# Preparing the inputs of the Strassen passes later in the plain steps

## The chip, the core and the metric
The kernel runs on one core of a Trainium2 chip. The metric is the device time of one execution in microseconds (us). The engines are called PE (TensorE matrix multiply), DVE (VectorE), ACT (ScalarE), POOL (GpSimd) and SP (SyncE, which here only issues transfers); PEld is the weight load of TensorE.

## The reference, cut to what matters
An attention block is followed by two feed-forward layers. The change lies in the second one, on 2304 tokens with 512 features and 1536 hidden columns:

```python
def _moe2_ref(x, w_gate, w_val, w_out, rms_g) -> np.ndarray:
    rms = np.sqrt(np.mean(x * x, axis=-1, keepdims=True) + 1e-06)
    xn = x / rms * rms_g
    g = xn @ w_gate
    silu = g * (1.0 / (1.0 + np.exp(-g)))
    val = xn @ w_val
    return (silu * val @ w_out).astype(np.float32)
```

## The kernel before, in words
Every product is made of three matmuls on split numbers: each operand is a high part (a cast on ACT) and a low part (a subtraction on DVE). Weights arrive as raw words (`raw`), are put together by two ACT operations (L184, L186) and one of DVE (L196, `ct`), and are then split into high (L203, ACT) and low (L207, DVE), tile `w`.

The second layer begins with a **plain part**, a loop over f = 0 to 11 (line 1385 and below), one step for each 128 hidden columns, on the first 256 tokens. A step prepares weights two steps ahead (`st2.to`), multiplies the 256 tokens by the gate and the value weight of step f (`pe_gv`: 12 matmuls each into `ps_h`), makes the activation (`s`, then its high and low part `p`: L949 ACT, L950 DVE, L952 ACT, L953 DVE), and adds the product with the output weight of step f - 2 (`pe_o`: 6 matmuls into `ps_x`).

The other 2048 tokens go through **Strassen passes** on sums and differences of weights. Their token inputs are seven tiles `xt`, one per product, numbered 1, 2, 5, 6, 3, 7, 4. A call of the generator `pg` in the plain loop runs `conv` for one of them: for numbers 5, 6, 7 and 4 a subtraction on DVE (L1039, `tr`, 128 x 1024), then for each a cast on ACT (L1058) and a subtraction on DVE (L1059). The same plain steps start the weight sums for the passes (`decode`): loads `wa`, sums `ws` on POOL (L302) and their split `wo` on POOL (L285, L286). The first pass reads tile 1 (`ps_pr<-xt,wt`) near the end of the plain part.

Who goes first is decided in two ways. From the last attention group on, transfers on SP go out in the order of the program. The instructions of PE, DVE, ACT and POOL in the plain part are put in order by the scheduler of the framework when the program is built: it plays the program through on its own estimate of times and takes, on each engine, the ready instruction that stands earliest in the program, unless `tc.high_priority` moves one forward (the activation of each step has it). On the chip every engine then keeps that order.

Of the kernel before, what the change touches and what calls it, by code (L numbers as in the profile page):

```python
# [34 lines left out]
def attn_moe_moe_kernel(  # L35
# [25 lines left out]
    B, _, NC, D = q_str.shape  # L61
    NT, DM = out.shape
    FA = w_in.shape[0]
    FB = w_gate.shape[0]
# [16 lines left out]
    def runs(s):  # L81

        r = []
        for i, (b, t) in enumerate(subs[s]):
            if r and r[-1][0] == b and r[-1][1] + r[-1][2] == t:
                r[-1][2] += 64
            else:
                r.append([b, t, 64, 64 * i])
        return r
# [36 lines left out]
    for s in range(len(subs)):  # L126
        if len(runs(s)) > 1 or s in LANES:
            _, t0, n, _ = runs(s)[0]
# [808 lines left out]
    def pe_gv(j, f):  # L937
        r, n = [], R0
        bank = (bank_h, bank_m, bank_h, bank_m, bank_x, bank_x)[f % 6]("ps_h")
        for k, kd in enumerate(("gate", "val")):  # L940
            ps = bank[:, k * n:k * n + n]
            w, x = w2[kd, f].t, xn[j]
            seq = [(a, e, c) for c in range(4) for a, e in ((0, 0), (0, 1), (1, 0))]
            for i, (a, e, c) in enumerate(seq):
                mm(ps, w[:, a, c, :], x[:, e, c, :], i == 0, i == len(seq) - 1)
            r.append(ps)
        with tc.high_priority(400):
            s = pb.tile([128, n], F32, tag="s", name="s", bufs=3)
            nc.scalar.activation(out=s, in_=r[0], func=ACTF.Silu, scale=WS)  # L949
            nc.vector.scalar_tensor_tensor(out=s, in0=r[1], scalar=WS, in1=s, op0=ALU.mult, op1=ALU.mult)  # L950
            t = pb.tile([128, 2, n], F32R, tag="p", name="p", bufs=3)
            nc.scalar.copy(out=t[:, 0], in_=s)  # L952
            nc.vector.tensor_tensor(out=t[:, 1], in0=s, in1=t[:, 0].bitcast(F32), op=ALU.subtract)  # L953
        p_of[j, f] = t

    def pe_o(j, f):
        if f == 0:
            oacc[j] = [ps_x.tile([128, 512], F32, tag="x", name="ps_x") for _ in range(R0 // 128)]
        w, p = w2["out2", f].t.rearrange("p s c f -> p s (c f)"), p_of.pop((j, f))
        for t in range(R0 // 128):  # L960
            for i, (a, e) in enumerate(((0, 0), (1, 0), (0, 1))):
                mm(
                    oacc[j][t], p[:, e, t * 128:t * 128 + 128], w[:, a, :],
                    f == 0 and i == 0, f == FB - 1 and i == 2,
                )
# [422 lines left out]
    for f in range(FB):  # L1388
        if f == FB - 4:
            pairs[0].fetch((0, 1))  # L1390
        st2.to(max(3 * (f + 2), N1 + (len(w2_order) - N1) * (f + 1) // (FB - 2)))
        store.plain(st2.i - 1)
        store.to(st2.i - 6)
        pe_gv(0, f)
        for _ in range(3 if f < FB - 2 else 40):
            next(pg, None)
        decode.to(max(0, min(8, 8 * (f - 4) // 6)))
        if f > 1:
            pe_o(0, f - 2)
# [155 lines left out]
```

## Time and profile before

| what | us |
|---|---|
| median of 3 runs (lowest, highest) | 886.05 (885.49, 890.01) |
| the profiled execution, its own time | 887.88 |
| its span in the trace | 886.1 |
| PE busy in that span | 866.5 |

The mean clock granted to PE over the span is 0.992 of full. Times in the rows below are microseconds from the start of the span. A busy PE is not PE at its peak, since matmuls overlap; what counts is where PE stood idle, and what it waited for. The plain part lies at about 470 to 522 us.

### The profile page before, as it was taken

The page shows a single profiled execution, that of the slowest core. Times are in us where ns is not written, and L with a number is a line of the kernel's source. Part 1 is how long each engine was busy: PE and PEld are TensorE (multiplying, and loading weights), DVE is VectorE, ACT ScalarE, POOL GpSimd, SP SyncE. Part 2 cuts the span into 40 slices and gives each one's busy share as a digit, 9 for nine tenths or more (in the row PEclk, how much of TensorE's full clock was granted, in tenths as well). Part 3 has the DMA queues.
Part 4 walks back from the last instruction along what each step waited for, and adds up shares of the span by engine and source line. Part 5 has one row for each costly group of instructions (what it writes and reads, how often), then busy time and mean ns, then how long its engine had stood idle before and what let it go on. Part 6 is the DMA issues. An engine that isn't in the chain of part 4 may idle for free.

```text
span 886.1 us, 14047 instructions
## 1 busy us (share of the span) xinstructions
PE 866.5 (98%) x5091; PEld 722.7 (82%) x5091; DVE 629.8 (71%) x1290; ACT 413.9 (47%) x916; POOL 250.6 (28%) x309
## 2 busy tenths in 40 slices
PE   7999999999999999999999899999999999999998
PEld 4888888888998887888889877888788888888886
DVE  5999778888779887657778945569688553445544
ACT  6887633333543333878657644533325324322230
POOL 0000147695366853000000679846200000000000
PEclk8999999999999999999999999999999999999999
DMA  9965224311313000889977999765661288544002
GB/s 302 368 223 178 74 75 156 104 57 36 115 55 110 25 19 27 330 306 370 412 252 227 352 372 336 299 230 214 211 216 48 75 320 353 177 149 136 1 1 95
DMA packets 63717, 164.12 MB, mean 185 GB/s; under 512 B 10080, under 2 KB 21728, under 8 KB 63648
## 3 DMA queue, kind: packets, MB, share of 16 engines
q1 hardware_dynamic: 61088, 159.56, 51.1%
q10 hardware_dynamic: 2560, 3.67, 1.2%
q8 instruction: 40, 0.66, 0.3%
q14 instruction: 29, 0.24, 0.1%
HBM read 119.16 MB, written 44.04 MB: 184 GB/s over the span
## 4 chain that ended last, share of the span: by engine, by line
PE 58%; DVE 10%; POOL 7%; issue 2%; ACT 2%; DMA 1%; SPq 0%; ACTq 0%; DVEq 0%; POOLq 0%
PE ps_pr L150 20%; PE ps_o L150 14%; PE ps_h L150 10%; PE ps_x L150 9%; POOL pr L675 5%; DVE so L715 4%; PE ps_q L150 4%; POOL pr L708 1%; DVE tg L860 1%; DVE g L871 1%; DMA wt<-w 1%; DMA w<-w 1%; DVE s L1108 0%; DVE sm L451 0%; POOL ws L302 0%
## 5 line engine op out<-in xcount | busy, mean ns | idle before, releaser
L150 PE MATMUL ps_h<-xs,w 128*128 128x512 f32 (+1 forms) x984 | 214.6, 367 | 0.7 <-DVE tg L860 0.7
L150 PE MATMUL ps_x<-g,w 128*128 128x512 f32 (+1 forms) x984 | 214.2, 366 | 0.0
L150 PEld LDWEIGHTS ps_h<-xs,w 128*128 128x128 f32 x984 | 169.9, 190 | 30.5 <-DVE tg L860 1.3
L150 PEld LDWEIGHTS ps_x<-g,w 128*128 128x128 f32 x984 | 168.5, 189 | 30.4 <-ACT g L866 0.4
L150 PE MATMUL ps_pr<-xt,wt 128*128 128x512 f32 x576 | 137.6, 390 | 2.0 <-DVE s L1118 1.1
L150 PE MATMUL ps_o<-wt,p 128*128 128x512 f32 x576 | 136.0, 389 | 0.0
L150 PEld LDWEIGHTS ps_pr<-xt,wt 128*128 128x128 f32 x576 | 107.7, 188 | 26.2 <-DVE s L1118 2.0
L150 PEld LDWEIGHTS ps_o<-wt,p 128*128 128x128 f32 x576 | 108.1, 188 | 22.5
L675 POOL TENSOR_TENSOR pr<-sk,sq 128x256 f32<-128x256 f32 (+2 forms) x101 | 82.6, 852 | 133.0 <-DMA sq<-in_q_str_dram 107.3
L866 ACT CAST g<-tg 128x512 fp32r<-128x512 f32 (+1 forms) x82 | 46.5, 567 | 101.3 <-DVE tg L860 101.2
L1129 ACT COPY u<-ps_pr 128x512 f32<-128x512 f32 x72 | 41.9, 587 | 103.5 <-PE ps_pr L150 103.4
L708 POOL TENSOR_TENSOR pr<-sv,se 128x288 f32<-128x288 f32 (+12 forms) x104 | 69.7, 691 | 57.0 <-DVE so L715 19.8
L1181 DVE SCALAR_TENSOR_TENSOR osum<-ps_o,osum 128x512 f32<-128x512 f32 x80 | 54.8, 687 | 27.2 <-PE ps_o L150 26.6
L302 POOL TENSOR_TENSOR ws<-wa 128x256 f32<-128x256 f32 x24 | 24.6, 1044 | 170.4 <-DVE w L207 152.2
L715 DVE TENSOR_REDUCE so<-pr 128x16 f32<-128x272 f32 (+11 forms) x104 | 64.9, 653 | 9.0 <-POOL pr L708 8.6
L150 PE MATMUL ps_pr<-xt,wo 128*128 128x512 f32 x288 | 67.4, 389 | 0.0
L150 PEld LDWEIGHTS ps_pr<-xt,wo 128*128 128x128 f32 x288 | 54.1, 188 | 11.3
L871 DVE TENSOR_TENSOR g<-tg,g 128x512 fp32r<-128x512 f32 (+1 forms) x82 | 55.3, 676 | 10.6 <-ACT g L866 9.3
L860 DVE SCALAR_TENSOR_TENSOR tg<-ps_h,tg 128x512 f32<-128x512 f32 (+1 forms) x82 | 50.6, 618 | 15.9 <-ACT tg L855 15.6
L855 ACT ACTIVATE tg<-ps_h 128x512 f32<-128x512 f32 (+1 forms) x82 | 44.2, 540 | 34.8 <-PE ps_h L150 34.7
L196 DVE SCALAR_TENSOR_TENSOR ct<-ca,ct 128x512 uint32<-128x512 uint32 x68 | 48.0, 713 | 16.6 <-ACT ca L186 16.0
L680 DVE TENSOR_REDUCE sc<-pr 128x4 f32<-128x256 f32 (+2 forms) x101 | 43.7, 437 | 12.1 <-POOL pr L675 11.7
(121 smaller groups left out, 1045.7 us busy)
## 6 DMA issues: line engine op xcount, KB each, us to landing
wt<-w SPq DMA_DIRECT2D x84, 512.0 KB, 4.6
w<-w SPq DMA_DIRECT2D x36, 512.0 KB, 6.2
raw<-in_w_out_dram SPq DMA_DIRECT2D x28, 512.0 KB, 5.8
w<-wo SPq DMA_DIRECT2D x24, 512.0 KB, 7.4
raw<-in_w_in_dram SPq DMA_DIRECT2D x16, 512.0 KB, 8.6
raw<-in_w_gate_dram SPq DMA_DIRECT2D x12, 512.0 KB, 6.7
raw<-in_w_val_dram SPq DMA_DIRECT2D x12, 512.0 KB, 7.1
wa<-v SPq DMA_DIRECT2D x24, 256.0 KB, 4.7
```

Source lines behind the costliest of these rows:

```text
L150: nc.tensor.matmul(out_, lhsT, rhs, start=start, stop=stop, skip_group_check=True)
L196: nc.vector.scalar_tensor_tensor(out=t, in0=self.a.bitcast(U32), scalar=3, in1=t, op0=ALU.logical_shift_left, op1=ALU.bitwise_or)
L675: nc.gpsimd.tensor_tensor(out=pr, in0=self.k[:, a:e, :], in1=self.q[:, c - c0:c - c0 + 1, :].to_broadcast([128, e - a, D]), op=ALU.mult,)
L680: pend.append(lambda: nc.vector.tensor_reduce(out=s[:, c - c0, a:e], in_=pr, axis=AX.X, op=ALU.add))
L708: nc.gpsimd.tensor_tensor(out=pr, in0=self.v[:, 0:c + 1, a:e], in1=self.e[:, c - c0, 0:c + 1].unsqueeze(2).to_broadcast([128, c + 1, e - a ...
L715: pend.append(lambda: nc.vector.tensor_reduce(out=o[:, c - g0, a:e], in_=pr.rearrange("l c d -> l d c"), axis=AX.X, op=ALU.add))
L855: nc.scalar.activation(out=t, in_=h_of[g, f, a], func=ACTF.Tanh, scale=WS)
L860: nc.vector.scalar_tensor_tensor(out=t, in0=h_of.pop((g, f, a)), scalar=WS, in1=t, op0=ALU.mult, op1=ALU.subtract)
L866: nc.scalar.copy(out=t[:, 0], in_=t_of[g, f, a])
L871: nc.vector.tensor_tensor(out=t[:, 1], in0=t_of.pop((g, f, a)), in1=t[:, 0].bitcast(F32), op=ALU.subtract)
L1129: nc.scalar.copy(out=u, in_=x[kd])
L1181: nc.vector.scalar_tensor_tensor(out=o, in0=ps, scalar=WS, in1=o, op0=ALU.mult, op1=ALU.add)
```

## The change
In each of the plain steps 0, 1 and 2 the loop called `next(pg)` three times, so all seven `conv` (the last two calls found nothing left) were in the program there. Now steps 0 to 3 call it not at all, step 4 twice (numbers 1 and 2) and steps 5 to 9 once (5, 6, 3, 7, 4). No instruction is added or removed; what moves is the place of 18 of them in the program, and with it the order that the scheduler finds.

```diff
         pe_gv(0, f)
-        for _ in range(3 if f < FB - 2 else 40):
+        for _ in range((f >= 4) + (f == 4) if f < FB - 2 else 40):
             next(pg, None)
         decode.to(max(0, min(8, 8 * (f - 4) // 6)))
```

The next two pieces are the order on DVE behind the L1059 of `xt1` and `xt2`, at about 483 us of the program before. Gate and value weight of step 7 are `w_5773` and `w_5778` before, `w_5765` and `w_5770` now; `xt_5706` is the tile shared by the numbers 3 and 7; `tr` are the differences. Before:

```order
L1039 TENSOR_TENSOR tr_5815<-x2_5239,tr_5762 128x1024
L1039 TENSOR_TENSOR tr_5821<-x2_5239 128x1024
L1059 TENSOR_TENSOR xt_5706<-x2_5239,xt_5706 128x1024
L207 TENSOR_TENSOR w_5773<-ct_5721,w_5773 128x512
L196 SCALAR_TENSOR_TENSOR ct_5827<-ca_5829,ct_5827 128x512
L1059 TENSOR_TENSOR xt5_5703<-tr_5762,xt5_5703 128x1024
L950 SCALAR_TENSOR_TENSOR s_5973<-ps_h_5948,s_5973 128x256
L207 TENSOR_TENSOR w_5778<-ct_5768,w_5778 128x512
L196 SCALAR_TENSOR_TENSOR ct_5877<-ca_5879,ct_5877 128x512
L950 SCALAR_TENSOR_TENSOR s_6014<-ps_h_5989,s_6014 128x256
L1059 TENSOR_TENSOR xt6_5704<-tr_5815,xt6_5704 128x1024
L1059 TENSOR_TENSOR xt_5706<-tr_5821,xt_5706 128x1024
```

The same place on DVE of the changed program:

```order
L1059 TENSOR_TENSOR xt_5706<-x2_5239,xt_5706 128x1024
L207 TENSOR_TENSOR w_5765<-ct_5721,w_5765 128x512
L207 TENSOR_TENSOR w_5770<-ct_5760,w_5770 128x512
L950 SCALAR_TENSOR_TENSOR s_5952<-ps_h_5927,s_5952 128x256
L196 SCALAR_TENSOR_TENSOR ct_5809<-ca_5811,ct_5809 128x512
L1059 TENSOR_TENSOR xt5_5703<-tr_6003,xt5_5703 128x1024
L196 SCALAR_TENSOR_TENSOR ct_5856<-ca_5858,ct_5856 128x512
L950 SCALAR_TENSOR_TENSOR s_5997<-ps_h_5972,s_5997 128x256
L950 SCALAR_TENSOR_TENSOR s_6064<-ps_h_6039,s_6064 128x256
L953 TENSOR_TENSOR p_5955<-s_5952,p_5955 128x256
L207 TENSOR_TENSOR w_5861<-ct_5809,w_5861 128x512
```

The two `tr` and the two L1059 of numbers 6 and 7 are gone from here; the weights of steps 7 and 8 (`w_5861`, before `w_5882`) come earlier.

They stand further down, ahead of the weights of step 10, which are `w_6033` (gate) and `w_6087` (value) in the changed program. DVE of the changed program there:

```order
L1039 TENSOR_TENSOR tr_6070<-x2_5239,tr_6070 128x1024
L196 SCALAR_TENSOR_TENSOR ct_6021<-ca_6023,ct_6021 128x512
L953 TENSOR_TENSOR p_6188<-s_6185,p_6188 128x256
L1059 TENSOR_TENSOR xt4_5705<-tr_6070,xt4_5705 128x1024
L207 TENSOR_TENSOR w_6033<-ct_6021,w_6033 128x512
L950 SCALAR_TENSOR_TENSOR s_6231<-ps_h_6206,s_6231 128x256
L1039 TENSOR_TENSOR tr_6191<-x2_5239 128x1024
L953 TENSOR_TENSOR p_6234<-s_6231,p_6234 128x256
L196 SCALAR_TENSOR_TENSOR ct_6028<-ca_6030,ct_6028 128x512
L1059 TENSOR_TENSOR xt_5706<-tr_6191,xt_5706 128x1024
L207 TENSOR_TENSOR w_6087<-ct_6028,w_6087 128x512
```

The value weight of step 10 now has `s_6231` and `p_6234` (activation of step 9) ahead of it, and `tr` and `xt` of number 7 as its neighbours.

PE at the end of the plain part, before (`w_6046`, `w_6096` are the weights of step 10, `w_6161`, `w_6204` those of step 11, `p_6279` the activation of step 10, `w_6039` its output weight):

```order
L150 MATMUL ps_h_6251<-xn_5193,w_6096 128x256 x10
L150 MATMUL ps_x_5868<-w_5776,p_6195 128x512
L150 MATMUL ps_x_5867<-w_5885,p_6237 128x512 x2
L150 MATMUL ps_x_5868<-w_5885,p_6237 128x512 x2
L150 MATMUL ps_x_5867<-w_5885,p_6237 128x512
L150 MATMUL ps_x_5868<-w_5885,p_6237 128x512
L150 MATMUL ps_h_6294<-xn_5193,w_6161 128x256 x2
L150 MATMUL ps_pr_6342<-xt1_5701,wt_6143 128x512 x6
L150 MATMUL ps_x_5867<-w_6039,p_6279 128x512 x2
L150 MATMUL ps_x_5868<-w_6039,p_6279 128x512 x2
L150 MATMUL ps_h_6294<-xn_5193,w_6161 128x256 x10
```

PE of the changed program from the value weight of step 10 on (`w_6154` and `w_6201` are the weights of step 11):

```order
L150 MATMUL ps_h_6251<-xn_5193,w_6087 128x256 x12
L150 MATMUL ps_x_5846<-w_6026,p_6279 128x512 x2
L150 MATMUL ps_x_5847<-w_6026,p_6279 128x512 x2
L150 MATMUL ps_x_5846<-w_6026,p_6279 128x512
L150 MATMUL ps_x_5847<-w_6026,p_6279 128x512
L150 MATMUL ps_pr_6342<-xt1_5701,wt_6136 128x512 x6
L150 MATMUL ps_h_6294<-xn_5193,w_6154 128x256 x12
L150 MATMUL ps_pr_6349<-xt1_5701,wt_6138 128x512 x6
L150 MATMUL ps_h_6294<-xn_5193,w_6201 128x256 x12
```

The output product of step 10 follows directly on the matmuls whose result it needs (`p_6279` is made from `ps_h_6251`); before, 15 other matmuls stood between. The order of transfers on SP and on ACT's queue is the same in both programs.

## Rows read from the trace of the kernel before

**Rows 1.** The page: busy time and share of each engine.

```profile
PE 866.5 (98%) x5091; PEld 722.7 (82%) x5091; DVE 629.8 (71%) x1290; ACT 413.9 (47%) x916; POOL 250.6 (28%) x309
```

**Rows 2.** Waits of PE, 482 to 545: total us, times, longest.

```profile
PE ps_h L150 <- DVE w L207: 2.1, 2, 1.8
PE ps_x L150 <- ACT p L952: 1.8, 2, 1.4
```

**Rows 3.** Waits of PE from 545 to the end.

```profile
PE ps_pr L150 <- DVE s L1118: 0.4, 1, 0.4
```

**Rows 4.** Timeline of PE: start, us, instruction, count, idle before.

```profile
487.10 2.25 PE L150 MATMUL ps_h<-xn,w 128*128 128x256 f32 x14 [0.30 <-DVE w L207]
...
493.90 2.26 PE L150 MATMUL ps_h<-xn,w 128*128 128x256 f32 x12 [1.84 <-DVE w L207]
```

**Rows 5.** Windows: busy us of PE, PEld, DVE, ACT, POOL; clock; DMA share; GB/s.

```profile
491.90:493.90 2.00, 0.17 (x2) 0.00 (x0) 2.00 (x4) 0.41 (x2) 0.00 (x0) 1.00 1.00 297
493.90:496.10 2.20, 2.19 (x13) 2.20 (x14) 2.20 (x5) 1.61 (x4) 0.67 (x1) 0.69 1.10 366
496.10:498.50 2.40, 2.40 (x9) 1.86 (x8) 2.40 (x5) 2.12 (x3) 2.40 (x1) 0.57 0.88 243
498.50:502.00 3.50, 3.50 (x25) 3.14 (x24) 3.50 (x4) 2.52 (x5) 3.50 (x4) 1.00 1.02 398
```

**Rows 6.** The chain that ended last: start, us, engine, tile, count.

```profile
493.90 2.26 PE ps_h L150 x12
496.17 2.37 PE ps_x L150 x6
...
500.42 1.40 PE ps_x L150 x6
501.81 1.42 PE ps_h L150 x12
...
508.63 1.19 PE ps_h L150 x10
...
511.80 1.37 PE ps_pr L150 x6
```

**Rows 7.** Timeline of DVE, first to last of the stretch before POOL starts.

```profile
478.00 0.69 DVE L196 SCALAR_TENSOR_TENSOR ct<-ca,ct 128x512 uint32<-128x512 uint32 x1
...
490.57 2.35 DVE L1059 TENSOR_TENSOR xt<-tr,xt 128x1024 fp32r<-128x1024 f32 x2
...
493.17 0.68 DVE L207 TENSOR_TENSOR w<-ct,w 128x512 fp32r<-128x512 f32 x1
```

**Rows 8.** Timeline of POOL, its first row of the plain part.

```profile
495.43 4.71 POOL L302 TENSOR_TENSOR ws<-wa 128x256 f32<-128x256 f32 x2 [152.24 <-DVE w L207]
```

**Rows 9.** Timeline of DVE while POOL works.

```profile
499.47 1.76 DVE L1059 TENSOR_TENSOR xt<-tr,xt 128x1024 fp32r<-128x1024 f32 x1
501.15 1.23 DVE L207 TENSOR_TENSOR w<-ct,w 128x512 fp32r<-128x512 f32 x1
...
504.33 0.41 DVE L950 SCALAR_TENSOR_TENSOR s<-ps_h,s 128x256 f32<-128x256 f32 x1
...
505.48 0.95 DVE L953 TENSOR_TENSOR p<-s,p 128x256 fp32r<-128x256 f32 x1
506.36 1.22 DVE L207 TENSOR_TENSOR w<-ct,w 128x512 fp32r<-128x512 f32 x1
```

**Rows 10.** Timeline of PE, the last output product of the plain part.

```profile
519.98 1.66 PE L150 MATMUL ps_x<-w,p 128*128 128x512 f32 x6 [1.43 <-ACT p L952]
```

**Rows 11.** Timeline of ACT: the value weight of step 11.

```profile
512.79 0.77 ACT L184 ACTIVATE ct<-raw,colf 128x512 uint32<-128x512 uint16 x1 [1.24 <-DMA raw<-in_w_val_dram]
...
515.36 0.62 ACT L203 CAST w<-ct 128x512 fp32r<-128x512 f32 x1 [1.24 <-DVE ct L196]
```

**Rows 12.** Timeline of DVE: the same weight.

```profile
514.16 1.17 DVE L196 SCALAR_TENSOR_TENSOR ct<-ca,ct 128x512 uint32<-128x512 uint32 x1 [1.11 <-ACT ca L186]
516.02 1.02 DVE L207 TENSOR_TENSOR w<-ct,w 128x512 fp32r<-128x512 f32 x1 [0.69 <-ACT w L203]
```

## The prediction, made before the changed kernel ran
> **What bounds the kernel now.** The page comes first: PE is busy for 98% of the span [rows 1], so only its gaps can be won, and the waits of PE say where they are. From 545 us on they come to 0.4 us in all [rows 3]. In the stretch of the plain steps PE waits 2.1 us for the low parts of weights (`w`, L207 on DVE) and 1.8 us for the high part of activations [rows 2]. The timeline of PE places them: 0.30 us before 487.10 and 1.84 before 493.90 [rows 4], and 1.43 of the 1.8 before the last output product at 519.98 [rows 10]; the other 0.36 lies between the first two. The reader is to see that the first three sit where DVE is full and holds L1059 (`xt`) ahead of the wanted weight: 2.35 us for two of them at 490.57, and the low part for which PE stood idle only at 493.17 [rows 7].
>
> The windows show what follows on the long gap. PE did 0.17 us of work in the 2.0 us up to 493.90; in the next two windows the mean granted clock is 0.69 and 0.57, that is, partly at the lower level of 1.2 GHz instead of 2.4; from 498.5 on it is 1.00 again [rows 5]. The chain gives the price: 12 matmuls of 256 columns take 2.26 us there and 1.42 later, 6 of 512 take 2.37 and 1.40 later [rows 6]; 0.84 + 0.97 = 1.81 us.
>
> **What the change can win.** It moves `tr` and `xt` of numbers 6, 7 and 4 behind the weights of steps 7 and 8 on DVE. The scheduler still leaves `xt` 1, 2 and 3 at their place, so the change does only part of what its words say, but the three gaps lose their cause: neither the two `xt` of 2.35 us nor the two `tr` stand ahead of that weight any more. I let all three waits go, and the slow stretch with them: 0.30 + 0.36 + 1.84 + 1.81 = 4.31 us. Nothing if the gaps only move; 4.31 is the upper end.
>
> **What it gives back.** Four steps, in order of time.
>
> *DVE.* Between the `ct` at 478.00 [rows 7] and the end of the L207 that begins at 506.36, the value weight of step 10 [rows 9], DVE executes 38 instructions and not one of their timeline rows has idle time before it. The L207 ends at about 507.5, where the next row starts. Up to the same weight the changed order has 40: the same kinds, plus one `s` (0.41) and one `p` (0.88 from its start to the next, 505.48 to 506.36) [rows 9]. A full engine with 1.29 us more work is done at 508.8. Then PE runs the 10 matmuls left of its 12: 1.42 x 10/12 = 1.18, to 510.0. Before, the same 10 began at 508.63 and took 1.19, to 509.8 [rows 6]. So the 4.31 us are spent by here: PE arrives early and waits for step 10's weights.
>
> *A chain laid bare.* PE's order then has the output product of step 10 directly behind the matmuls whose result it needs. Before, 15 matmuls covered the activation. Its price is the row of the same chain without cover, 1.43 us [rows 10]: PE goes on at 511.4. Six `ps_x` (1.40) and six `ps_pr` (1.37) [rows 6] follow, to 514.2.
>
> *Weights of step 11.* In ACT's new order the two operations that open the gate weight stand behind the cast of that activation, so they start at 511.4. From first ACT operation to the end of L207, the value weight of step 11 took 512.79 to 516.02 + 1.02 = 517.04, 4.25 us [rows 11, 12]. The gate weight is ready at 511.4 + 4.25 = 515.65; PE, after two matmuls on the high part, waits from 514.4. With 10 matmuls and six `ps_pr` it is at 515.65 + 1.18 + 1.37 = 518.2. The value weight opens on ACT when the gate's high part is done, 515.36 + 0.62 - 512.79 = 3.19 us after 511.4, and needs 4.25 more: 518.85. PE's 10 last matmuls end at 520.0.
>
> *The last chain* is unchanged, 1.43: the last output product starts at 521.45 instead of 519.98. **Sum: 1.5 us later.** Where the chain of step 11's weights is counted at nothing, PE's own work is 1.40 + 1.37 + 1.42 + 1.37 + 1.42 with two chains of 1.43, 9.84 from 510.0, and ends at 519.8: 0.2 us earlier, the lower end of these three steps. Taking the 1.29 of DVE off as well gives 1.5 us earlier.
>
> Everything else I put at nothing. The change issues no transfer and keeps the order on SP and on ACT's queue; two ACT operations (0.8 us together) now precede the read that frees one raw buffer, so one load leaves 0.8 us later, covered by the weight's lead of a step, and by nothing in the last two steps, where the DMA engines are full anyway [rows 5]. The `xt` tiles are done before 509 by the same count and the pass reads all but number 1 after 521. Much later, three L994 go ahead of one L1118 on DVE; PE waits there for 0.4 us in all [rows 3], and the matmuls beside it cover it; without cover it would cost about 1 us.
>
> **A price that speaks against the change.** While POOL works, from 495.43 on [rows 8], DVE's instructions with two inputs in SBUF stretch: L207 from 0.68 to 1.23, L1059 from half of 2.35 to 1.76 [rows 7, 9], about 0.55 each. The changed order brings `xt` of numbers 6 and 7 and one `tr` into that time, but DVE is one queue: three short instructions (`ct`, `w`, `p`) leave it for earlier places, and each of them was stretched as well. So I take no net loss; if the long ones are stretched and nothing is saved, 3 x 0.55 = 1.6 us more. The Trainium skill, "SBUF — State Buffer", section "Who interferes with whom", says that a VectorE instruction with two SBUF inputs contends with a GpSimd instruction that reads SBUF, and that the later one fully blocks. By that rule an instruction would wait for the rest of whichever POOL instruction runs, whatever its own length, which the trace bears out (0.55 for the short and the long).
>
> **The rivals.**
> 1. *The gain is kept.* If DVE has slack that I don't see, PE keeps 4.31 us: 881.7. For it: the gaps do lose their cause. Against: 38 instructions without idle time. 0.08.
> 2. *DMA decides.* The last raw weight landed at 512.79 with ACT waiting 1.24 us for it [rows 11], and the DMA engines are busy at a share of about 1 for long before [rows 5], so it can't land earlier. If DVE and ACT are faster than I reckon, this weight ends at 517.04 again and the end stays where it was: 885.9. 0.15.
> 3. *POOL in the way:* the 1.6 us above come on top: 889.1. 0.10.
> 4. *The other side: the clock.* PE now stands idle for most of 504 to 508.8, longer than before 493.90, and the granted clock may fall again, and stay low because three more waits follow. At the lower level a stretch of 1.42 + 1.40 = 2.82 us cost 1.81 more [rows 6], 0.64 for each us. If all 7.0 us of matmuls that remain in the plain part run so, 4.5 us come on top of 1.5: 892.0. It decides, that is passes 0.5%, from (4.43 - 1.5) / 0.64 = 4.6 us of matmuls on. For it: the gap is longer. Against: before, the low level lasted for only 2.8 us' worth, and part of the delay falls into waits for step 11's weights. 0.12.
>
> **How the numbers follow.** The forecast has 0.55. The profiled execution took 887.88, 1.83 above the median of 886.05; by the sum it would take 889.4, and against the median 886.05 + 1.5 = 887.5. Less than 0.5% of the median, 4.4 us, can hardly be told from no change here; the three runs alone differ by 4.5. Faster than that needs rival 1 and a wait of the first pass removed too: 0.03. Slower needs most of rival 4: 0.08. Same: 0.89. The range leaves out rival 1 (0.08) and rival 4 where it is longest (0.1): from 884.5, which holds the 1.5 us of the lower bounds, to 890.0, which holds rival 3 with its end.
>
> **What would show it.** Right: no PE wait for L207 before 494 and a clock of 1.00 from 486 to 500; then waits for L207 that add up to some 4 us between 502 and 509; L207 of step 10's value weight ending near 508.8 with DVE full up to there; a wait of about 1.4 for `p` L952 near 511; a wait near 515 for the gate weight of step 11; the last output product at about 521.4. Wrong: DVE idle before 507, or that product before 519 or after 524; or the second half of the kernel, whose order hardly moves, changing by over 1 us.

## The result, and the profile after

| | us |
|---|---|
| kernel before, median of 18 | 886.54 |
| changed kernel, median of 18 (lowest, highest) | 890.75 (888.63, 895.95) |
| ratio, 95% interval | 1.0055, 1.0043 to 1.0067 |
| profiled execution of the changed kernel, its span | 889.48, 887.7 |

The forecast was 887.5, no change that can be told; the kernel became slower by 0.55%, just outside the range. The page of the changed kernel shows next to nothing of it, since PE is as busy as before [rows 1]:

```profile
PE 866.5 (98%) x5091; PEld 722.8 (81%) x5091; DVE 634.2 (71%) x1290; ACT 413.3 (47%) x916; POOL 248.3 (28%) x309
```

Two executions can't be laid side by side from the start of the span: the part ahead of the plain steps took 3.3 us less in the profiled execution of the changed kernel. So places are given from here on as their distance from one instruction that stands in both, the first `ct` (L196) behind the four L1025 on DVE; it began at 478.00 before and at 474.71 after. Three distances tell the story, each read off a timeline row:

| profile | value weight of step 10 done (DVE) | last output product begins (PE) | between the two | end of the span |
|---|---|---|---|---|
| before | 29.6 | 42.0 | 12.4 | 408.1 |
| forecast | 30.8 | 43.45 | 12.65 | 409.6 |
| changed | 31.9 | 47.2 | 15.3 | 413.0 |

The whole loss of 4.9 us between these two executions is in the plain steps; from the last output product to the end the two kernels take 366.1 and 365.75. Waits of PE in the plain steps of the changed kernel, from 482 to 545 (total, times, longest), the rows that answer to [rows 2]:

```profile
PE ps_h L150 <- DVE w L207: 2.8, 2, 1.4
PE ps_x L150 <- ACT p L952: 2.8, 2, 1.4
PE ps_h L150 <- ACT w L203: 1.1, 1, 1.1
```

Where they lie, and how long the matmuls behind them take, is in the timeline of PE. It answers to [rows 4, 6, 10]:

```profile
500.40 1.45 PE L150 MATMUL ps_h<-xn,w 128*128 128x256 f32 x10 [1.39 <-DVE w L207]
...
504.76 0.50 PE L150 MATMUL ps_h<-xn,w 128*128 128x256 f32 x2 [1.06 <-ACT w L203]
506.67 2.50 PE L150 MATMUL ps_h<-xn,w 128*128 128x256 f32 x10 [1.42 <-DVE w L207]
510.60 2.93 PE L150 MATMUL ps_x<-w,p 128*128 128x512 f32 x6 [1.43 <-ACT p L952]
513.33 2.76 PE L150 MATMUL ps_pr<-xt,wt 128*128 128x512 f32 x6
515.89 1.87 PE L150 MATMUL ps_h<-xn,w 128*128 128x256 f32 x12
...
521.95 1.66 PE L150 MATMUL ps_x<-w,p 128*128 128x512 f32 x6 [1.37 <-ACT p L952]
```

The reader is to see two things. The three gaps of before are gone, as foreseen, and four stand in step 10 instead: PE waits for the gate weight (1.39), then for the high and the low part of the value weight (1.06, 1.42), then for the activation (1.43). And ten matmuls of one form take 1.45 us at 500.40 and 2.50 at 506.67. The windows tell why (columns as in [rows 5], the clock third from the end):

```profile
502.90:504.80 1.90, 0.78 (x3) 0.34 (x3) 1.90 (x3) 1.02 (x2) 1.90 (x3) 1.00 1.02 416
504.80:506.60 1.80, 0.46 (x2) 0.25 (x2) 1.80 (x2) 0.00 (x0) 1.80 (x2) 0.91 1.03 394
506.60:508.50 1.90, 1.83 (x8) 1.83 (x9) 0.02 (x1) 0.00 (x0) 1.90 (x2) 0.50 1.07 414
...
513.30:515.90 2.60, 2.60 (x8) 1.99 (x7) 1.37 (x3) 1.85 (x3) 0.00 (x0) 0.50 0.28 103
515.90:517.60 1.70, 1.70 (x14) 1.70 (x12) 0.71 (x2) 0.62 (x1) 0.00 (x0) 0.82 0.87 305
```

From 506.6 to 515.9 the granted clock is 0.50, the lower of its two levels (1.2 GHz): over 9 us, against some 4.6 us of partly low clock before. DVE up to the value weight of step 10 (the L207 at 505.52), which answers to [rows 7, 9]:

```profile
491.67 1.23 DVE L1059 TENSOR_TENSOR xt<-tr,xt 128x1024 fp32r<-128x1024 f32 x1 [0.43 <-ACT xt L1058]
...
493.74 1.76 DVE L1039 TENSOR_TENSOR tr<-x,tr 128x1024 f32<-128x1024 f32 x1
...
497.47 1.75 DVE L1059 TENSOR_TENSOR xt<-tr,xt 128x1024 fp32r<-128x1024 f32 x1
...
500.27 0.41 DVE L950 SCALAR_TENSOR_TENSOR s<-ps_h,s 128x256 f32<-128x256 f32 x1
500.61 1.42 DVE L1039 TENSOR_TENSOR tr<-x 128x1024 f32<-128x1024 f32 x1
...
503.98 1.63 DVE L1059 TENSOR_TENSOR xt<-tr,xt 128x1024 fp32r<-128x1024 f32 x1
505.52 1.09 DVE L207 TENSOR_TENSOR w<-ct,w 128x512 fp32r<-128x512 f32 x1
```

The two `tr` and two `xt` of numbers 4 and 7 all lie in the time in which POOL works, from 493.63 on, and all are stretched. POOL's first row of the plain part, which answers to [rows 8]:

```profile
493.63 2.48 POOL L302 TENSOR_TENSOR ws<-wa 128x256 f32<-128x256 f32 x2 [153.70 <-DMA wa<-v]
```

DVE is not quite full in the changed kernel: ahead of the `xt` at 491.67 it stood idle for 0.43 us, waiting for a cast on ACT.

### The profile page after: what moved, and what is told of

Its sections match the earlier page's. It is cut to its first block, busy times and chain, and to the rows that moved or that the text cites. A ratio compares the mean times of both kernels' runs of the same rounds, so it can differ in the third digit from the quotient of the medians.

```text
span 887.7 us, 14050 instructions
## 1 busy us (share of the span) xinstructions
PE 866.5 (98%) x5091; PEld 722.8 (81%) x5091; DVE 634.2 (71%) x1290; ACT 413.3 (47%) x916; POOL 248.3 (28%) x309
## 4 chain that ended last, share of the span: by engine, by line
PE 56%; DVE 13%; POOL 7%; issue 3%; ACT 2%; DMA 1%; ACTq 0%; DVEq 0%; POOLq 0%
PE ps_pr L150 20%; PE ps_o L150 13%; PE ps_h L150 10%; PE ps_x L150 9%; POOL pr L675 5%; DVE so L715 4%; PE ps_q L150 3%; DMA v<-ct 1%; POOL pr L708 1%; DVE tg L860 1%; DVE g L871 1%; DVE s L1108 1%; DVE p L1113 1%; DVE osum L1181 0%; DVE sm L451 0%
## 5 line engine op out<-in xcount | busy, mean ns | idle before, releaser
L150 PEld LDWEIGHTS ps_h<-xs,w 128*128 128x128 f32 x984 | 168.7, 189 | 30.5 <-DVE tg L860 1.3
L1129 ACT COPY u<-ps_pr 128x512 f32<-128x512 f32 x72 | 41.9, 586 | 102.2 <-PE ps_pr L150 102.1
L302 POOL TENSOR_TENSOR ws<-wa 128x256 f32<-128x256 f32 x24 | 23.1, 983 | 175.2 <-DMA wa<-v 163.4
L196 DVE SCALAR_TENSOR_TENSOR ct<-ca,ct 128x512 uint32<-128x512 uint32 x68 | 48.7, 725 | 14.9 <-ACT ca L186 14.3
```

The lines of the kernel that those rows point to most:

```text
L150: nc.tensor.matmul(out_, lhsT, rhs, start=start, stop=stop, skip_group_check=True)
L196: nc.vector.scalar_tensor_tensor(out=t, in0=self.a.bitcast(U32), scalar=3, in1=t, op0=ALU.logical_shift_left, op1=ALU.bitwise_or)
L1129: nc.scalar.copy(out=u, in_=x[kd])
```

## The experiments

All are variants of the changed kernel unless a text says "before". The ratio is to the kernel before on the same chip, with its 95% interval; the last three columns are distances from the first `ct` in each one's profile (end = end of the span). A profile is one execution, and executions of one kernel differ by some us, so the ratio says how much, and the profile where.

| | median us | ratio (interval) | value weight of step 10 | last output product | end |
|---|---|---|---|---|---|
| before | 886.13 to 887.94 | 1 | 29.6 | 42.0 | 408.1 |
| changed | 890.75 | 1.0055 (1.0043, 1.0067) | 31.9 | 47.2 | 413.0 |
| e1, PE kept busy in step 10 | 890.63 | 1.0046 (1.0030, 1.0062) | 33.1 | 45.6 | 411.4 |
| e2, inputs from step 0, one a step | 888.80 | 1.0020 (1.0007, 1.0033) | 30.5 | 43.9 | 408.8 |
| e3, only numbers 7 and 4 late | 890.04 | 1.0035 (1.0023, 1.0046) | 31.8 | 44.4 | 410.0 |
| e4, sums four steps later | 893.68 | 1.0078 (1.0058, 1.0099) | 25.5 | 41.9 | 413.3 |
| e5, before with PE kept busy in step 8 | 886.78 | 1.0001 (0.9986, 1.0016) | 29.6 | 42.0 | 407.3 |
| e6, numbers 7 and 4 short on DVE | 889.14 | 1.0038 (1.0022, 1.0053) | 29.6 | 42.6 | 407.3 |
| e7, before with sums two steps later | 888.11 | 1.0021 (1.0001, 1.0041) | 25.6 | 42.2 | 409.5 |
| e8, sums two steps later | 886.26 | 0.9996 (0.9982, 1.0010) | 26.6 | 40.1 | 406.2 |
| e9, sums one step later | 887.52 | 0.9995 (0.9985, 1.0005) | 25.0 | 41.9 | 407.7 |
| e10, inputs from step 2, sums two later | 889.63 | 1.0024 (1.0014, 1.0034) | 25.5 | 42.6 | 410.2 |
| e11, the changed kernel again | 893.19 (one) | | 33.1 | 47.8 | 412.7 |
| e12, e6 with one cast moved to DVE | 888.39 (one) | | 30.4 | 43.5 | 409.1 |
| e13, e9 with PE kept busy | 886.54 | 0.9990 (0.9976, 1.0004) | 25.0 | 41.7 | 407.3 |
| e14, e1 again | 891.04 (one) | | 32.2 | 45.0 | 410.4 |

**e1: is it the clock?** 28 matmuls on a tile of zeros stand in PE's gaps of step 10; they add nothing to the sums, and the order of the rest stays.

```diff
+                if f == 10 and i == 2:
+                    for _ in range((10, 10)[k]):
+                        mm(ps, ones, zer, False, False)
                 mm(ps, w[:, a, c, :], x[:, e, c, :], i == 0, i == len(seq) - 1)
+            if f == 10 and k == 0:
+                for _ in range(8):
+                    mm(bank[:, n:2 * n], ones, zer, True, True)
```

> The changed kernel with 28 extra matmuls in step 10 (10 behind the first two of the gate product, 8 behind the gate product, 10 behind the first two of the value product). They multiply a tile of zeros, so they add nothing; the order on every engine stays that of the changed kernel. The clock theory (the gaps before step 10's weights let the granted clock fall to 0.50 until about 516 us, and the matmuls at that level cost 4 us): PE no longer stands idle between about 499 and 507, the clock stays at 1.00, and the time falls by 3 to 4 us from the changed kernel's, to 887 to 888. The rival (the late weights and the bare chain cost the time, and slow matmuls only fill what PE would have waited): no change, 890 to 891, whatever the clock does.

Its timeline of PE (lines behind the edit are 6 higher in this kernel):

```profile
513.24 1.45 PE L150 MATMUL ps_h<-xn,w 128*128 128x256 f32 x10 [0.90 <-DVE w L207]
516.11 1.65 PE L150 MATMUL ps_x<-w,p 128*128 128x512 f32 x6 [1.43 <-ACT p L958]
517.60 1.54 PE L150 MATMUL ps_pr<-xt,wt 128*128 128x512 f32 x6
...
525.74 1.66 PE L150 MATMUL ps_x<-w,p 128*128 128x512 f32 x6 [1.37 <-ACT p L958]
```

A window of e1, the one that holds the value weight:

```profile
510.00:514.00 4.00, 2.67 (x19) 2.25 (x19) 3.18 (x2) 0.60 (x1) 4.00 (x3) 1.00 1.05 406
```

The clock stays at 1.00, and from the value weight (513.18) to the last output product it is 12.55 us instead of 15.3: the fallen clock costs 2.8 us there. But the median fell by only 0.1 us, the ratio by 0.0009 (0.8 us), against 3 to 4 expected. The two intervals overlap, and 890.63 lies where the rival of the expectation put it (890 to 891, whatever the clock does). In this execution the value weight itself came 1.2 us later. e11 and e14 take that up.

**e2 and e3: which inputs?**

```diff
-        for _ in range((f >= 4) + (f == 4) if f < FB - 2 else 40):
+        for _ in range((2, 1, 1, 1, 1, 1)[f] if f < 6 else 40 if f >= FB - 2 else 0):    e2
+        for _ in range((3, 2, 0, 0, 0, 0, 0, 0, 1, 1)[f] if f < FB - 2 else 40):         e3
```

> The seven inputs given to the scheduler two in step 0 and one in each of steps 1 to 5. On DVE the weights of step 7 still come ahead of the subtractions of numbers 5, 6 and 7, but all seven inputs are through before step 9's weights. If it is the inputs of numbers 7 and 4 among the weights of steps 9 and 10, while POOL works, that make PE wait there: no long wait in step 10, clock at 1.00 throughout, 884 to 886. If any move of inputs behind weights costs what the change costs: 889 to 891.

> Numbers 1, 2, 5, 6 and 3 in steps 0 and 1 as before, number 7 in step 8 and number 4 in step 9 as in the changed kernel. If the two late ones make the loss: PE waits for step 10's weights again, the clock falls to 0.50 after it, 889 to 891. If number 6 or the earlier ones do: as the kernel before, 886 to 887.

e2 lost 0.2%, where a gain was expected: a gap of 2.48 us came back at step 8 (there for `p` L953), and 1.57 us of bare activation chain later. e3 leaves five inputs where they were before and moves only numbers 7 and 4; its time was as expected, but its clock never fell. Two windows of e3:

```profile
506.00:510.00 4.00, 1.99 (x9) 1.35 (x8) 4.00 (x5) 1.02 (x2) 4.00 (x4) 1.00 1.02 409
510.00:514.00 4.00, 2.45 (x14) 2.02 (x15) 1.36 (x3) 1.84 (x4) 4.00 (x5) 1.00 0.74 285
```

So the two late inputs alone bring the value weight of step 10 as late as the whole change does (31.8), with the bare chain behind it, and that cost 0.35% although this execution shows no loss of clock.

**e4: the sums out of the way.** The weight sums on POOL are given four steps later.

```diff
-        decode.to(max(0, min(8, 8 * (f - 4) // 6)))
+        decode.to(max(0, min(8, 8 * (f - 8) // 3)))
```

> The changed kernel with the weight sums on POOL begun in step 9 instead of step 5. If POOL stretches DVE's instructions by about 0.5 us each: L207 takes 0.69 again up to step 10, and step 10's value weight is done 3 to 4 us earlier after the first ct than in the changed kernel, so PE does not wait there. The first pass then waits for the sums; the time is 887 to 893, by how much of POOL's 18 us no longer lies under the plain steps. If POOL does not matter: the same waits in step 10 as the changed kernel.

DVE of e4 at the place where it was stretched:

```profile
498.92 1.21 DVE L1059 TENSOR_TENSOR xt<-tr,xt 128x1024 fp32r<-128x1024 f32 x1
500.06 0.68 DVE L207 TENSOR_TENSOR w<-ct,w 128x512 fp32r<-128x512 f32 x1
500.66 0.41 DVE L953 TENSOR_TENSOR p<-s,p 128x256 fp32r<-128x256 f32 x1
```

These are the durations without POOL: 1.21, 0.68 and 0.41 instead of 1.75, 1.20 and 0.96. The value weight comes at 25.5. But POOL begins at 514.95, the first pass waits for its sums (1.90 us for `wo` in the waits of PE), and the part behind the last output product takes 371.4 us instead of 366. The scheduler also laid the inputs early again, with the gap of step 8 back, so e4 parts nothing cleanly; its time, 893.68, lies just above the range of its expectation.

**e5: what was the slow clock of before worth?** Ten matmuls on zeros in the kernel before, inside the gate product of step 8; the rest of the order stays.

```diff
+                if f == 8 and k == 0 and i == 2:
+                    for _ in range(10):
+                        mm(ps, ones, zer, False, False)
```

> The kernel before with 10 matmuls on a zero tile inside the gate product of step 8, behind its first two, where TensorE stands idle for 1.84 us; the order of all other instructions stays. It tells what the slow clock behind that gap costs before. Clock theory: the gap shrinks to some 0.7, the clock stays at full, the 1.81 us of slow matmuls come back; PE is at most 0.9 us behind the value weight of step 10 there (507.58 against 508.47), so not all is kept: 885.0 to 886.0, last output product about 41 us behind the first ct instead of 41.98. Rival (VectorE decides, the clock is free): 886.5 to 887.2, last output product at 42.0 or later.

PE of e5:

```profile
492.90 1.69 PE L150 MATMUL ps_h<-xn,w 128*128 128x256 f32 x12 [1.28 <-DVE w L207]
...
505.25 0.50 PE L150 MATMUL ps_h<-xn,w 128*128 128x256 f32 x2 [0.34 <-ACT w L203]
...
510.29 0.50 PE L150 MATMUL ps_h<-xn,w 128*128 128x256 f32 x2 [0.57 <-ACT w L203]
...
518.97 1.66 PE L150 MATMUL ps_x<-w,p 128*128 128x512 f32 x6 [1.43 <-ACT p L955]
```

The clock is held: 12 matmuls take 1.69 us, not the 2.26 of [rows 6]. PE is 1.55 us earlier at the next step, and gives it back: two waits that before didn't have (0.34, 0.57) and gaps too short for a row, and the last output product stands at 42.0 again. The rival was right. The kernel before lost nothing that can be told by its slow clock, since the value weight of step 10 (29.6) and the high part of step 11's gate weight (33.2 in both) come no earlier.

**e6 and e12: DVE's time, or the order?** In e6 the four DVE instructions of numbers 7 and 4 do 128 of 1024 columns, each at its place. This leaves out part of the computation: the passes read the high part of these two inputs in place of the low one, and the cast on ACT reads a token tile, so it no longer waits for the difference (`tr`).

```diff
+            z = 64 if name in ("t3", "t4") else HT
-            nc.vector.tensor_tensor(out=out, in0=p, in1=q, op=ALU.subtract)
+            nc.vector.tensor_tensor(out=out[:, :, :z], in0=p[:, :, :z], in1=q[:, :, :z], op=ALU.subtract)
...
+        z = 64 if m in (7, 4) else HT
-        nc.scalar.copy(out=t[:, 0], in_=v)
+        nc.scalar.copy(out=t[:, 0], in_=b[1, 1] if z < HT else v)
...
```

> The changed kernel in which the four VectorE instructions of the numbers 7 and 4 that stand ahead of step 10's weights do 128 of their 1024 columns, each at its place; the passes read the high part of these two inputs instead of the low one, so this leaves out part of the computation. Theory that VectorE's work there is what is late: these four took 6.25 us in the trace, some 1.0 us is left, so the value weight of step 10 comes 4 to 5 us earlier (27 to 28 us behind the first ct instead of 31.9), the waits in step 10 go, the clock does not fall, and the time is 885.0 to 887.0. Rival, the clock alone: 888. Rival, the bare chain and the weights of step 11 decide: 889.5 to 891.

The ratio fell from 1.0055 to 1.0038, a third of the loss, where all of it was expected; the two intervals overlap, and the profile (end at 407.3) is of the fastest execution of e6 and does not show the loss. The clock fell here too: six `ps_x` behind step 10's weights take 2.93 us. The value weight came 2.3 us earlier, not 4 to 5, for two reasons. The four short instructions were stretched as well and took 2.75 us (0.29, 0.85, 0.83, 0.78) instead of 6.56, so that 3.8 us of DVE's time went and not 5; and something else now held the weight. ACT of e6:

```profile
502.44 0.39 ACT L949 ACTIVATE s<-ps_h 128x256 f32<-128x256 f32 x1 [2.02 <-PE ps_h L150]
503.94 0.41 ACT L952 CAST p<-s 128x256 fp32r<-128x256 f32 x1 [1.11 <-DVE s L950]
504.25 0.76 ACT L184 ACTIVATE ct<-raw,colf 128x512 uint32<-128x512 uint16 x1
```

The value weight of step 10 opens (L184) only behind the activation of step 9, and that waits for PE. In the kernel before the same L184 ran at 500.79, directly behind the `s` of step 8 and ahead of that step's cast, let alone of step 9:

```profile
500.51 0.38 ACT L949 ACTIVATE s<-ps_h 128x256 f32<-128x256 f32 x1 [0.31 <-PE ps_h L150]
500.79 0.75 ACT L184 ACTIVATE ct<-raw,colf 128x512 uint32<-128x512 uint16 x1
...
504.78 0.41 ACT L952 CAST p<-s 128x256 fp32r<-128x256 f32 x1 [2.67 <-DVE s L950]
```

In the changed kernel it stands behind the cast of step 9 (500.72):

```profile
501.03 0.76 ACT L184 ACTIVATE ct<-raw,colf 128x512 uint32<-128x512 uint16 x1
```

From the first `ct` that is 22.8 us before, 26.3 in the changed kernel and 25.5 in e6. PE's value product of step 9 ends at 23.6 in both of the latter; from there to the finished weight it is 8.3 us in the changed kernel and 6.0 in e6. e12 takes the cast of step 9 off ACT:

```diff
-            nc.scalar.copy(out=t[:, 0], in_=s)
+            (nc.vector.tensor_copy if f == 9 else nc.scalar.copy)(out=t[:, 0], in_=s)
```

> The kernel with the two late inputs short (which leaves out part of the computation), and the high cast of step 9's activation done on VectorE instead of ACT; no other instruction changes its place. In the kernel with short inputs ACT opened step 10's value weight at 504.25, directly behind that cast at 503.94, 1.5 us behind the start of s on ACT. If ACT's order is the second bound under VectorE's, the value weight opens 1.2 to 1.5 us earlier against the first ct (24 instead of 25.5) and its low part ends 1 us earlier (28.6 instead of 29.6); if the raw weight or a buffer holds it, nothing moves.

The weight opened 1.25 us earlier, as expected (501.81, which is 24.3), but was done 0.8 us later, not 1 us earlier: on DVE, too, `ct` stands behind `s`, the cast and `p` of step 9. So ACT's order alone isn't the second bound; the weight stands behind the activation on both engines, and this run doesn't part them.

**e7, e8, e9, e10: the sums somewhat later.**

```diff
-        decode.to(max(0, min(8, 8 * (f - 4) // 6)))
+        decode.to(max(0, min(8, 8 * (f - 6) // 5)))    e7 (before), e8, e10
+        decode.to(max(0, min(8, 8 * (f - 5) // 5)))    e9
-        for _ in range((f >= 4) + (f == 4) if f < FB - 2 else 40):
+        for _ in range((f >= 2) + (f == 2) if f < FB - 2 else 40):    e10
```

> The kernel before with the weight sums of GpSimd given about two steps later (8 * (f - 6) // 5 in place of 8 * (f - 4) // 6). In the kernel before PE does not wait for VectorE between 494 and 519, so less stretch on VectorE gains nothing there: 886.0 to 887.5 by the theory that only what PE waits for counts; if the sums come too late for the first pass (it reads wo right behind the last output product), 888 to 890. Rival, that GpSimd's overlap costs time before as well: 884 to 885.5.

> The changed kernel with the same later sums. If GpSimd's stretch of VectorE is a main part of the late weights of step 10, the value weight comes 2 to 4 us earlier than 31.9 us behind the first ct, the waits in step 10 shrink, and the time is 885.5 to 888.0; no long gap before 494 stands against it. If the late numbers 4 and 7 alone decide, 889.5 to 891. If the first pass then waits for wo, as it did with the sums put later still: 889 to 892, with a PE wait for wo near 525.

> The changed kernel with the sums given one step later (8 * (f - 5) // 5), between the changed kernel (890.75) and the one with the sums two steps later (886.26). If what counts is that GpSimd's work starts behind step 10's weights, this one lies between, 887 to 889, with the value weight of step 10 some 28 to 30 us behind the first ct; if it counts more that wo is ready early for the first pass, which ran at the slow clock for 2 us in the two-step version, it beats both: 884.5 to 886.

> Sums two steps later, and the inputs given from step 2 on (two, then one a step) instead of from step 4. The inputs are then done before step 10's weights, and the long gap of the kernel before should not be back in full, since only one input a step is ahead of a weight. 884.5 to 886.5 if VectorE's order in steps 7 to 10 is what costs; 886.5 to 888.5 if a gap at step 8 comes back with its slow clock.

In the kernel before later sums cost 0.2%, just more than can be told from nothing: DVE had its value weight 4 us earlier, and PE did not need it (the waits for L207 and L952 in e7 are those of before, and the last output product stands at 42.2). What this execution lost lies behind it, where 367.3 us pass instead of 366.1. The first twelve `ps_pr` there take 4.01 us instead of 2.91, with the granted clock at 0.67 from 520 to 524; but e8 has them at 3.81 and still takes only 366.0, so this is not shown to be the loss. In the changed kernel the same edit, and that of e9, wins the whole loss back, 0.9996 and 0.9995. POOL and DVE in e8:

```profile
505.08 1.44 POOL L302 TENSOR_TENSOR ws<-wa 128x256 f32<-128x256 f32 x2 [161.72 <-DMA wa<-v]
```

```profile
502.89 1.23 DVE L1059 TENSOR_TENSOR xt<-tr,xt 128x1024 fp32r<-128x1024 f32 x1 [0.28 <-ACT xt L1058]
504.03 0.69 DVE L207 TENSOR_TENSOR w<-ct,w 128x512 fp32r<-128x512 f32 x1
```

The value weight is done at 504.72, ahead of POOL's first instruction, at full speed; and ACT opened it at 498.89, ahead of the `s` of step 9 at 501.53. So this edit takes away both, the stretch and the order, and doesn't say which of them counted for more. e10, with the inputs two steps earlier, loses 0.24%: PE waits for 2.49 us before a `ps_x` at 493.61, the place of the old gap, and six `ps_x` behind it take 2.34 us, as at the lower clock: the second case of its expectation in kind, though 889.63 lies above that range too. e9's value weight came at 25.0, earlier than the 28 to 30 expected, and the kernel neither lies between the two nor beats them.

**e11 and e14: does the clock fall each time?**

> The changed kernel once more, for a second profile: does the clock fall behind the waits of step 10 in every execution? If it does, the granted clock is about 0.5 for some 7 to 9 us of the stretch between the value weight of step 10 and the end of the plain part, and the way from that weight to the last output product is again about 15.3 us; if it falls in some executions only, about 12.5 us, and the median of many executions holds less of it than the one profile.

> The changed kernel with filling matmuls in step 10 once more, for a second profile. The value weight of step 10 came 31.9 and 33.1 us behind the first ct in two profiles of the changed kernel and 33.1 in the first of this one; if the difference is scatter, it lies between 31.5 and 33.5 here, with the clock at 1.00 and 12.5 us from it to the last output product.

Windows of the second execution of the changed kernel:

```profile
509.00:511.00 2.00, 0.50 (x2) 0.30 (x2) 2.00 (x2) 0.23 (x1) 2.00 (x2) 0.77 1.03 395
511.00:513.00 2.00, 1.15 (x5) 1.15 (x6) 0.80 (x1) 0.00 (x0) 2.00 (x3) 0.50 1.06 414
...
517.00:519.00 2.00, 2.00 (x7) 1.54 (x6) 1.31 (x2) 1.26 (x3) 0.00 (x0) 0.50 0.27 99
```

It fell again and stayed low for some 9 us; value weight to last output product 14.7 us, and the value weight itself at 33.1 instead of 31.9, so that place scatters by over 1 us between executions of one kernel. More than half of this is the last instruction, which takes 1.75 us here and 1.09 in the first execution, with POOL at work in both:

```profile
510.05 1.75 DVE L207 TENSOR_TENSOR w<-ct,w 128x512 fp32r<-128x512 f32 x1
```

e14, the filled kernel, has 32.2 and then 12.9, with the clock at 1.00. Over two profiles each, the last output product stands at 47.5 in the changed kernel and at 45.3 in the filled one: holding the clock is worth 2.2 us in these profiles, and 0.8 in the ratios, give or take 1.8 (from their two intervals, 0.0012 and 0.0016 of 887).

**e13: a version that beats both?** e9 with ten matmuls on zeros ahead of the output product of step 10; nothing else moves.

```diff
-        w, p = w2["out2", f].t.rearrange("p s c f -> p s (c f)"), p_of.pop((j, f))
+        w, p, z = w2["out2", f].t.rearrange("p s c f -> p s (c f)"), p_of.pop((j, f)), [mm(oacc[j][0][:, :256], ones, zer, False, False) for _ in range(10 * (f == 10))]
```

> The changed kernel with the sums one step later and 10 matmuls on a zero tile ahead of the output product of step 10, where PE waited 1.30 and 0.65 us and the granted clock fell (six ps_pr took 2.56 us there instead of 1.38). No other instruction moves. If the clock is worth what the rows say, 1.2 us of ps_pr and 0.4 around it come back, less what the weights of step 11 hold: 0.5 to 1.6 us under the version without filling, ratio 0.998 to 0.9989 to the kernel before, which would beat both. If the raw weight of step 11 decides the end, 0.9995 again.

PE of e13 behind the filling:

```profile
509.27 1.20 PE L150 MATMUL ps_x<-w,p 128*128 128x512 f32 x4
511.13 0.73 PE L150 MATMUL ps_x<-w,p 128*128 128x512 f32 x2 [0.66 <-DVE p L953]
511.70 1.55 PE L150 MATMUL ps_pr<-xt,wt 128*128 128x512 f32 x6
513.48 0.50 PE L150 MATMUL ps_h<-xn,w 128*128 128x256 f32 x2 [0.23 <-ACT w L203]
514.53 1.46 PE L150 MATMUL ps_h<-xn,w 128*128 128x256 f32 x10 [0.54 <-DVE w L207]
```

Six `ps_pr` take 1.55 us at the full clock, not the 2.76 of e9, and two waits for the weights of step 11 (0.23, 0.54) take most of it back: the last output product moves by 0.2 us. The ratio, 0.9990, can't be told from 1. No version here beats the kernel before by more than its measurement can tell.

## Why the prediction was wrong, step by step

**What the change wins: half right.** The three waits went, 2.50 us, and the clock stays at 1.00 from 494.7 to 504.8. But the 1.81 us of slow clock that I counted as won brought nothing: e5 takes them away in the kernel before, and gains nothing that can be told.

**"DVE": the first failed step, right in kind and mis-sized by 1.1 to 2.3 us.** PE came early and waited for step 10's weights, 1.39, 1.06 and 1.42 us where I had said some 4 together. The value weight was forecast at 30.8 and came at 31.9 (33.1 in a second execution; 33.1 and 32.2 in the filled kernel, whose order is the same). Between the first profile (31.9) and the kernel before (29.6) lie 2.3 us: 0.7 for the `s` and `p` at full speed, 1.1 for more stretch, and 0.5 at the `xt` of 491.67, where DVE waited for a cast on ACT. The 1.29 us of the forecast held the 0.7 and one stretch, that of the `p`. So about half of the missing 1.1 us is the price that I named in "A price that speaks against the change" and then took as nothing, and half is a wait that "a full engine" left no room for. The stretch is counted as follows. In the changed kernel the 11 instructions from 493.74 to the end of the L207 at 506.61 take 12.87 us; with the distances from start to start of e4 (1.13 for `tr`, 1.14 for `xt`, 0.60 for `ct` and `w`, 0.33 for `s` and `p`, 0.68 for the last L207 to its end) they would take 8.0, so the stretch is 4.9 us. Before, nine instructions from 498.65 to 507.51 took 8.86 instead of 5.1: 3.7. The changed order puts ten stretched two-input instructions ahead of the weight instead of eight, and they lose just under 0.5 us each on the mean (0.2 to 0.56). That short ones leave that time did not make up for it, because before they were not stretched there: POOL began at 495.43, but DVE's five rows from 495.64 to 498.65 kept their full speed, and POOL's first two L302 took 4.71 us instead [rows 8]. The first of the five, of the kernel before:

```profile
495.64 1.22 DVE L1039 TENSOR_TENSOR tr<-x,tr 128x1024 f32<-128x1024 f32 x1
```

In the changed kernel POOL's first two took 2.48, and DVE was stretched from the first. The Trainium skill, "SBUF — State Buffer", section "Who interferes with whom", has a VectorE instruction with at most one input in SBUF, outside its 2-port modes, free of this contention; the trace agrees, since `s`, with one input in PSUM, takes 0.41 us with POOL at work and without.

**"A chain laid bare" and "Weights of step 11": the second failed step, in the profiles.** Their working puts all of PE's matmuls behind step 10's weights at the full clock, 12.65 us from the value weight to the last output product. It took 15.3 and 14.7 in two executions, and 12.55 and 12.9 where PE was kept busy. The chain itself cost 1.43, as foreseen. The wait near 515 for step 11's gate weight did not come, since PE, at half the clock, got there after it. This is the mechanism of rival 4, to which I gave 0.12. I argued that part of the delay lies in waits. The clock was low for 9 us and its net price was 2.7 us, not 4.5: the four groups of matmuls in that time took 3.8 us more than those of e1 (2.50, 2.93, 2.76 and 1.87 against 1.45, 1.65, 1.54 and 1.59), so by the difference 1.1 of it stands where PE would have waited. With 1.1 for DVE it makes 3.8 us, the distance from the forecast 43.45 to 47.2. Where the clock was held, in e1 and e14, the last output product begins 1.9 us behind the forecast on the mean, and nearly all of that is the weight: 32.6 instead of 30.8, and then 12.7 us.

**The rivals.** The gain was not kept (rival 1). That DMA decides the end (rival 2) is not borne out in either kernel. In the changed one ACT opens the value weight of step 11 at 513.86 without waiting for its transfer. In e5 it is opened at 510.45, 1.3 us earlier against the first `ct` than before and again without that wait, and the last output product stays at 42.0; what PE waited for there (0.34, 0.57) is step 10's value weight and step 11's gate weight. Rivals 3 and 4 came together, and I had priced them one at a time.

**The rest at nothing: right.** Behind the last output product the changed kernel takes 365.75 us, the one before 366.1.

**What I did not see** is the order that e6 laid open: the value weight of step 10 stands behind the activation of step 9 on ACT and on DVE. The order shown ahead of the prediction has it on DVE, and I read it as 1.29 us of work. It is a ring: PE's value product of step 9, its activation, the weight of step 10, PE. Taking 3.8 us of other work off DVE in e6 freed the weight by 2.3 us.

**Open.** How the loss divides between stretch, order and clock in the median is not settled: the clock is worth 2.2 us in profiles and 0.8 +- 1.8 in ratios, e1 with the clock held still loses 0.46% where the forecast stood for 0.17, e6 leaves two thirds of the loss with most of the late inputs' time taken away, and e8 and e9 undo stretch and order at once. What is shown is that the late numbers 4 and 7 alone suffice for most of the loss (e3: 0.35 of 0.55%), and that it goes when the sums are given later (e8, e9), with the scheduler's order changed as well.

## What to carry to other kernels

Work moved out of one gap goes in front of the next consumer of the same engine: count there what it costs with the contention of that place (POOL at work), not of the place that it left. A slow clock or a gap is only worth winning if what PE needs next is there earlier too; test that by filling the gap with matmuls on zeros before moving anything. And where a weight stands behind an activation on the engines that prepare it, PE waits for its own product, and lighter work on either engine helps only in part (2.3 us for 3.8 in e6): look for that ring in the order, not in busy shares.

## What was not expected of the hardware

The granted clock fell at different sums of waits. In the changed kernel waits of 1.39, 1.06 and 1.42 us within 8 us were followed by 9 us at 0.50; in the first window at that level PE was busy for 1.83 of 1.90 us. In e3 waits of 0.63, 1.41, 0.73 and 1.43 us within 10 us left it at 1.00. Before, a gap of 1.84 us was followed by 4.6 us at 0.69 and 0.57 [rows 5]. No rule that would part these three cases was tried.
